# An attention and MoE kernel: the first loads in another order with filler matmuls, block means of v from two rows to a partition, q loaded in halves

## The chip, the core and the metric

The kernel runs on one core of a Trainium2 chip. The metric is device time in microseconds (us) of one execution. The core has four engines that compute (PE is TensorE, DVE is VectorE, ACT is ScalarE, POOL is GpSimd) and SyncE (SP), whose queue issues every load and store of this kernel to 16 DMA engines. Each engine takes its own instructions in a fixed order and waits where data or a buffer isn't ready.

## What is computed

Attention of 2 batches, 8 heads, 768 positions and 64 columns, in which a query sees the 31 keys around it and, for the rest, the 24 blocks of 32 keys: per block the maximum of k and the mean of v. Then two MoE-like layers on the 1536 tokens:

```python
k_sum = k.reshape(B, H, nb, block, D).max(axis=3)
v_sum = v.reshape(B, H, nb, block, D).mean(axis=3)
...
scores_s = scores_s + np.log(block)
...
scores_all = np.concatenate([scores_l_m, scores_s], axis=-1)
a = softmax(scores_all)
attn = np.matmul(a, np.concatenate([v, v_sum], axis=2))
# x: the attention's output, 1536 tokens x 512
h = x @ w_in                      # 512 -> 1024
x = layer_norm(h * softmax(h)) * g_ln @ w_out
h = x @ w_in2                     # 512 -> 2048
out = elu(h) @ w_out2
```

## The kernel before

The attention is done in 24 steps n (batch b, tile t of 64 queries, 12 tiles to a batch). For a step, `attn_s(n)` multiplies `q_bd[n]` (two heads on the diagonal of a 128 x 128 block, the other half zeros, so one matmul serves two heads) with the key window `kws[n % 4]` (96 keys and the 24 block maxima), adds a mask and takes the softmax: the sum with the mask and the minimum on DVE, the exponential on ACT, the scaling on POOL. `attn_p(n)` turns the result with PE transposes, and `attn_x(j)` multiplies the steps 2j and 2j+1 with their v windows `vws[n % 4]` (96 rows of v and the 24 block means) into `xT[j]`, 128 tokens for the first layer. `mm_in(j, n)` then runs the first layer's half n for these tokens: 4 slices of w_in, each with three matmuls (high parts, high by low, low by high), 12 matmuls to a half, written below as h(j, n). They need `xT[j]` and the slices of w_in, which arrive as 64-bit words and are turned into two 32-bit floats each by `convert`: ACT, POOL, DVE, DVE, ACT, DVE, one after the other; there are 8 slices, 0 to 3 for half 0, 4 to 7 for half 1. `lo_of`, the last DVE step of `convert` and of `split`, makes the low part; for `xT` it does so from PSUM.

The block maxima of k come from DVE reductions (`sum_k`), of batch 1 too. The block means of v come from matmuls (`sum_v`): six tiles of 128 rows of v, 512 columns in 32-bit floats, each multiplied with a slice of `avg` that puts four means in their rows; ACT brings the 24 x 512 result to `vsum`, and POOL copies it into each of the four v windows. Batch 1's v rows are loaded to a buffer that batch 0's v rows held before, and batch 1's keys (`load_k(1)`) go to that same buffer when the second `sum_v` has read it.

The order on SP is that of the program text (`manual_schedule`). PE, DVE, ACT and POOL are put in order by a scheduler at build time, which the text steers with priorities. SP has eight semaphores for its DMAs, taken in turn, so a load waits for the eighth one before it. In the beginning, 32 matmuls on zeros (`busy`) run while the first loads come.

## Time and profile before

| | us |
|---|---|
| median of 3 runs | 480.14 (479.35 to 481.42) |
| the profiled execution | 480.95 |
| its span, from the first to the last instruction | 479.2 |
| PE busy in the span | 464.0 (97%) |
| DVE, ACT, POOL busy | 298.6, 286.9, 122.3 |

The profiled execution's own time is 1.75 us over its span, and 0.81 us over the median. PE is busy for nearly the whole span, but the first instants hold fillers: the first matmul with data in it starts at 11.40 us.

### The profile page before, as it was taken

Reading aid. Unit: us, or ns where it says so; the run is one execution under the profiler, and the core shown is the slowest. Engines: PE = TensorE matmul, PEld = TensorE weight load, DVE = VectorE, ACT = ScalarE, POOL = GpSimd, SP = SyncE. Lnnn points to the kernel's source line nnn. Section 1 sums busy time; section 2 is a strip of 40 time slices with the busy share of each in tenths; the row PEclk is TensorE's granted clock in tenths of the full one; section 3 lists DMA queues with packets and bytes.
Section 4 is the critical chain, followed back from the end, with each engine's and each line's share of the span. In section 5 each row is a group of like instructions: output and inputs, shape, how many; then the busy total and the mean of one; then the engine's idle time right before and its main releaser. Section 6 shows DMA issues by size and latency. Waiting matters only on the chain.

```text
span 479.2 us, 7413 instructions
## 1 busy us (share of the span) xinstructions
PE 464.0 (97%) x2600; PEld 390.1 (81%) x2600; DVE 298.6 (62%) x664; ACT 286.9 (60%) x647; POOL 122.3 (26%) x213
## 2 busy tenths in 40 slices
PE   7789999899999999999999999999999999999996
PEld 3456788789988989999888888888888888888885
DVE  3786779885568529786998893367665565450000
ACT  1795697986568428475957673567667666560001
POOL 2795276755443512332222200000000000000000
PEclk9999999999999999999999999999999999999999
DMA  8996995462280543388879614442212222377112
GB/s 284 353 365 185 297 299 174 127 193 77 84 256 19 166 133 130 118 291 315 244 273 385 213 54 136 172 175 60 72 51 83 88 60 73 133 297 274 44 44 88
DMA packets 40116, 82.46 MB, mean 172 GB/s; under 512 B 9616, under 2 KB 18448, under 8 KB 40080
## 3 DMA queue, kind: packets, MB, share of 16 engines
q1 hardware_dynamic: 40080, 82.00, 52.1%
q8 instruction: 20, 0.33, 0.3%
q14 instruction: 16, 0.13, 0.1%
HBM read 70.46 MB, written 11.53 MB: 171 GB/s over the span
## 4 chain that ended last, share of the span: by engine, by line
PE 86%; DMA 8%; DVE 3%; ACT 1%; SPq 1%; issue 0%
PE o_ps L110 9%; PE o_ps L108 9%; PE o_ps L109 9%; PE h L110 7%; PE h L108 7%; PE h L109 7%; PE c L110 5%; PE c L108 5%; PE c L109 5%; DMA q_bd<-in_qd 5%; PE y_ps L108 5%; PE y_ps L110 5%; PE y_ps L109 5%; PE s_ps L218 3%; PE t_ps L299 2%; DMA vw<-in_v 2%
## 5 line engine op out<-in xcount | busy, mean ns | idle before, releaser
L129 POOL TENSOR_SCALAR conv<-conv 128x512 f32<-128x512 f32 x48 | 37.6, 785 | 81.2 <-ACT conv L126 79.6
L232 POOL TENSOR_SCALAR sm<-sm,st 128x120 f32<-128x120 f32 x96 | 43.8, 472 | 30.7 <-DVE st L230 14.3
L108 PE MATMUL o_ps<-w4r,g_hl 128*128 128x512 f32 x128 | 49.8, 389 | 0.0
L109 PE MATMUL o_ps<-w4r,g_hl 128*128 128x512 f32 x128 | 49.8, 389 | 0.0
L110 PE MATMUL o_ps<-w4r,g_hl 128*128 128x512 f32 x128 | 46.7, 389 | 0.0
L108 PE MATMUL y_ps<-lnT,w_out 128*128 128x384 f32 x128 | 43.6, 341 | 0.8 <-ACT y L316 0.8
L227 ACT ACTIVATE sm<-sm,st 128x120 f32<-128x120 f32 x96 | 37.0, 390 | 10.7 <-DVE st L224 10.7
L109 PE MATMUL y_ps<-lnT,w_out 128*128 128x384 f32 x128 | 43.2, 337 | 0.0
L110 PE MATMUL y_ps<-lnT,w_out 128*128 128x384 f32 x128 | 42.9, 336 | 0.0
L108 PE MATMUL h<-w_in,xT 128*128 128x512 f32 x96 | 39.3, 411 | 0.8 <-ACT xT L138 0.8
L110 PE MATMUL h<-w_in,xT 128*128 128x512 f32 x96 | 38.5, 401 | 0.8 <-DVE xT L105 0.8
L109 PE MATMUL h<-w_in,xT 128*128 128x512 f32 x96 | 38.4, 400 | 0.0
L224 DVE CUSTOM_DVE_ANT_0 sm<-s_ps,mask 128x120 f32<-128x120 f32 x96 | 21.6, 277 | 14.6 <-PE s_ps L218 14.2
L593 ACT ACTIVATE y<-y 128x512 f32<-128x512 f32 x48 | 30.0, 628 | 0.7
L621 DVE COPY y<-o_ps 128x512 f32<-128x512 f32 x5 | 3.5, 690 | 42.9 <-PE o_ps L110 42.9
L623 ACT ACTIVATE y<-o_ps 128x512 f32<-128x512 f32 x6 | 3.6, 600 | 43.9 <-PE o_ps L110 43.9
L105 DVE TENSOR_TENSOR g_hl<-y,g_hl 128x512 fp32r<-128x512 f32 x32 | 22.4, 701 | 11.3 <-ACT g_hl L138 11.2
L218 PE MATMUL s_ps<-kw,q_bd 128*128 128x120 f32 x192 | 25.9, 278 | 3.6 <-DMA q_bd<-in_qd 3.1
L218 PEld LDWEIGHTS s_ps<-kw,q_bd 128*128 128x128 f32 x192 | 23.9, 191 | 6.5 <-POOL kw L101 1.9
L109 PEld LDWEIGHTS o_ps<-w4r,g_hl 128*128 128x128 f32 x128 | 24.1, 188 | 5.1
L126 ACT ACTIVATE conv<-y 128x512 f32<-128x512 f32 x30 | 20.2, 676 | 13.3 <-DMA y<-in_w_in 11.3
L110 PEld LDWEIGHTS o_ps<-w4r,g_hl 128*128 128x128 f32 x128 | 24.0, 188 | 5.0
(148 smaller groups left out, 1239.9 us busy)
## 6 DMA issues: line engine op xcount, KB each, us to landing
w4r<-w4d SPq DMA_DIRECT2D x38, 512.0 KB, 3.4
y<-in_w_in SPq DMA_DIRECT2D x16, 512.0 KB, 5.9
w4d<-w3f SPq DMA_DIRECT2D x16, 512.0 KB, 3.4
y<-in_w_out SPq DMA_DIRECT2D x14, 512.0 KB, 7.0
q_bd<-in_qd SPq DMA_DIRECT2D x24, 256.0 KB, 7.0
bits<-in_w_out SPq DMA_DIRECT2D x10, 512.0 KB, 5.0
w4l<-w4d SPq DMA_DIRECT2D x10, 512.0 KB, 4.6
vw<-in_v SPq DMA_DIRECT2D x24, 192.0 KB, 6.5
```

The lines of the kernel that those rows point to most:

```text
L105: nc.vector.tensor_tensor(out_, x, hi.bitcast(F32), op=ALU.subtract)
L108: nc.tensor.matmul(ps, lhsT=l[0][ls], rhs=r[0][rs], start=first, stop=False, skip_group_check=parts)
L109: nc.tensor.matmul(ps, lhsT=l[0][ls], rhs=r[1][rs], start=False, stop=False, skip_group_check=parts)
L110: nc.tensor.matmul(ps, lhsT=l[1][ls], rhs=r[0][rs], start=False, stop=last, skip_group_check=parts)
L126: first = nc.scalar.activation(x, high.bitcast(F32), AF.Prelu, scale=TO_F32, alpha=SIGN_TO_28)
L129: nc.gpsimd.tensor_scalar(x, x, MOST, LEAST, op0=ALU.min, op1=ALU.max)
L218: nc.tensor.matmul(sps[:, p, 0:KW], lhsT=q_bd[n][:, p, :], rhs=kw[:, p, :], start=True, stop=True)
L224: nc.vector.tensor_tensor_reduce(sm[:, p, :], sps[:, p, 0:KW], mask[:, mi, :], -scale, 3.0e38, op0=ALU.add, op1=ALU.min, accum_out=nm[:, p ...
L227: nc.scalar.activation(sm[:, p, :], sm[:, p, :], AF.Exp, bias=nm[:, p:p + 1], scale=-1.0, accum_out=ss[:, p:p + 1])
L232: nc.gpsimd.tensor_scalar(sm[:, p, :], sm[:, p, :], ri[:, p:p + 1], 1.0, op0=ALU.mult, op1=ALU.mult)
L299: nc.tensor.transpose(tp[:, i, :], es[j][:, k * 128:(k + 1) * 128], ident)
L593: nc.scalar.activation(m, m, AF.Exp, scale=-1.0)
```

## The change

- **Loads.** SP's first loads are put in another order: batch 0's keys, q of step 0, the mask, q of step 1, then slices of w_in, v windows, `ident`, `avg` and v's rows between each other. Loading and converting a slice of w_in are now two functions (`words_w_in`, `convert_w_in`), and their places in the text are apart. `load_k(1)` stands two steps later in tick 1, behind the loads of that tick.
- **q.** The four q buffers are fixed tiles, whose zero halves VectorE writes once (8 memsets of 64 x 256). From step 2 on only the two non-zero quarters of a q block are loaded, as two DMAs of 64 partitions with runs of 64 floats (256 bytes) in place of one DMA with runs of 2 KB.
- **Means.** v's rows are loaded in three DMAs of 256 rows, two rows to a partition (runs of 4 KB) and not in six with runs of 2 KB; `avg` is loaded to match. Batch 0 still takes six matmuls. In batch 1 VectorE adds the two rows of each pair first (three additions of 128 x 512), and three matmuls are left. Batch 0's means go from PSUM straight into the first two v windows, one by ACT and one by DVE; POOL copies only into the other two.
- **Fillers.** 12 more matmuls on zeros follow the scores of step 1, and 7 follow `attn_x(0)`.

```diff
     def sum_v(b):
-        pst = psb.tile([128, DM], F32, tag="b", name="vs_ps")
...
-        for i in range(S // 128):
-            vt = v_sb[:, i * DM:(i + 1) * DM]
-            nc.sync.dma_start(vt, v[b, PAD + i * 128:PAD + (i + 1) * 128, :])
-            c0 = NB - i * 4
-            nc.tensor.matmul(pst, lhsT=avg[:, c0:c0 + 128], rhs=vt, start=i == 0, stop=i == S // 128 - 1)
-        vsum[b] = p_at.tile([128, DM], F32, tag="vsum", name="vsum", bufs=1)
-        nc.scalar.activation(vsum[b][WIN:KW, :], pst[WIN:KW, :], AF.Copy)
+        vts = [v_sb[:, i * 2 * DM:(i + 1) * 2 * DM].rearrange("p (s d) -> p s d", s=2) for i in range(S // 256)]
+        for i, vt in enumerate(vts):
+            nc.sync.dma_start(vt, v[b, PAD + i * 256:PAD + (i + 1) * 256, :].rearrange("(p s) d -> p s d", s=2))
+
+        def products():
+            pst = psb.tile([128, DM], F32, tag="b", name="vs_ps")
+            for i, vt in enumerate(vts):
+                c0 = NB - i * 8
+                if b:
+                    nc.vector.tensor_tensor(vt[:, 0], vt[:, 0], vt[:, 1], op=ALU.add)
+                for s in range(2 - b):
+                    nc.tensor.matmul(pst, lhsT=avg[:, c0:c0 + 128], rhs=vt[:, s], start=i + s == 0,
+                                     stop=i == S // 256 - 1 and s == 1 - b)
+            vsum[b] = p_at.tile([128, DM], F32, tag="vsum", name="vsum", bufs=1) if b else vws[0]
+            nc.scalar.activation(vsum[b][WIN:KW, :], pst[WIN:KW, :], AF.Copy)
+            if b == 0:
+                nc.vector.tensor_copy(vws[1][WIN:KW, :], pst[WIN:KW, :])
+        return products
...
     def load_q(n):
-        q_bd[n] = p_at.tile([128, NP, 2 * TQ], F32, tag="q", name="q_bd", bufs=4)
-        nc.sync.dma_start(q_bd[n], qd[n])
+        q_bd[n] = qs[n % NQ]
+        if n < 2:
+            nc.sync.dma_start(q_bd[n], qd[n])
+            return
+        for hh in range(2):
+            ds, cs = slice(hh * D, (hh + 1) * D), slice(hh * TQ, (hh + 1) * TQ)
+            nc.sync.dma_start(q_bd[n][ds, :, cs], qd[n, ds, :, cs])
...
+    keep_busy(32)
...
+    keep_busy(12, attn_s(1))
+    for i in range(2):
+        with tc.issue_after(marks[1, "max"].ins), tc.issue_after(marks[i, "exp"].ins):
+            convert_w_in(i)
+    means()
...
+    keep_busy(7, attn_x(0))
     attn_s(3)
...
         if t == 0:
-            sum_v(1)
-        elif t == 1:
-            load_k(1)
+            sum_v(1)()
...
             load_kw(s_n + 1)
+            if t == 1:
+                load_k(1)
             attn_s(s_n)
```

What this does to the engines' orders is seen best in the instructions as built. First SP's queue from its start, before; q_bd stands for the q of step 1 and then of step 0, vw_121 for the first v window, y_65 and y_66 for the places where slices of w_in arrive:

```order
L171 DMA k_sb<-in_kT 128x800 x4
L194 DMA q_bd<-in_qd 128x512
L198 DMA vw_121<-in_v 96x512
L474 DMA mask<-in_mask 128x360
L476 DMA ident<-in_ident 128x128
L194 DMA q_bd<-in_qd 128x512
L117 DMA y_65<-in_w_in 128x1024
L479 DMA avg<-in_avg 128x152
L117 DMA y_65<-in_w_in 128x1024
L186 DMA v_sb<-in_v 128x512 x6
L117 DMA y_66<-in_w_in 128x1024 x2
L194 DMA q_bd<-in_qd 128x512
```

And the same place in the changed kernel, where q_bd_126 to q_bd_129 are the four q buffers:

```order
L506 DMA avg<-in_avg 64x152
L507 DMA avg<-in_avg 64x148
L196 DMA v_sb<-in_v 128x1024 x3
L124 DMA y_66<-in_w_in 128x1024
L224 DMA vw_122<-in_v 96x512
L124 DMA y_66<-in_w_in 128x1024
L220 DMA q_bd_128<-in_qd 64x4x64 x2
L220 DMA q_bd_129<-in_qd 64x4x64 x2
L224 DMA vw_123<-in_v 96x512
L124 DMA y_67<-in_w_in 128x1024
```

The q of step 2 (q_bd_128) has moved behind the second v window and comes in two DMAs, the one of step 3 follows at once; ahead of this piece stand the keys, both first q, the mask, two slices of w_in, one v window and `ident`.

Next PE where the means of batch 1 are made, before. s_ps are scores, p_ps transposes, h the first layer, x_ps the product with v, kw_119 the key window of step 6:

```order
L188 MATMUL vs_ps<-v_sb,avg 128x512 x2
L108 MATMUL h<-w_in_89,xT 128x512
L188 MATMUL vs_ps<-v_sb,avg 128x512
L109 MATMUL h<-w_in_90,xT 128x512
L110 MATMUL h<-w_in_89,xT 128x512
L188 MATMUL vs_ps<-v_sb,avg 128x512 x3
L108 MATMUL h<-w_in_89,xT 128x512
L218 MATMUL s_ps<-kw_119,q_bd 128x120 x4
L254 MATMUL x_ps<-pT,vw_124 64x64 x8
```

And after:

```order
L205 MATMUL vs_ps<-v_sb,avg 128x512
L116 MATMUL h<-w_in_90,xT 128x512
L117 MATMUL h<-w_in_89,xT 128x512
L265 MATMUL p_ps<-ident,sm 120x128 x3
L205 MATMUL vs_ps<-v_sb,avg 128x512
L115 MATMUL h<-w_in_89,xT 128x512
L244 MATMUL s_ps<-kw_119,q_bd_128 128x120 x4
L205 MATMUL vs_ps<-v_sb,avg 128x512
L116 MATMUL h<-w_in_90,xT 128x512
L117 MATMUL h<-w_in_89,xT 128x512
L282 MATMUL x_ps<-pT,vw_124 64x64 x8
```

Three products are left of six, and the last of them now stands behind the scores of step 6.

Last DVE at the same place after the change, where L203 are the additions of v's pairs, L112 on w_in_90 the end of a slice's conversion, L137 and L141 steps of the next slices:

```order
L203 TENSOR_TENSOR v_sb<-v_sb 128x512
L112 TENSOR_TENSOR w_in_90<-conv,w_in_89 128x512
L137 TENSOR_SCALAR conv<-conv 128x512
L203 TENSOR_TENSOR v_sb<-v_sb 128x512
L141 SCALAR_TENSOR_TENSOR conv<-y_65,conv 128x512
L255 TENSOR_SCALAR st<-st 128x4
```

The three additions have come in between the conversions of slices 5, 6 and 7; the third stands behind the minimum of step 4's scores.

## Rows read from the trace of the kernel before

**Rows 1.** The page's first part: busy us, share of the span, instructions.
```profile
PE 464.0 (97%) x2600; PEld 390.1 (81%) x2600; DVE 298.6 (62%) x664; ACT 286.9 (60%) x647; POOL 122.3 (26%) x213
```
**Rows 2.** Busy us by stages; behind the engines the clock, DMA share, GB/s.
```profile
10.00:26.70 16.70, 11.76 (x84) 7.92 (x85) 11.46 (x48) 11.60 (x38) 13.36 (x25) 1.00 1.05 367
26.70:46.50 19.80, 17.76 (x115) 12.66 (x115) 14.23 (x50) 13.80 (x44) 15.78 (x29) 1.00 0.77 258
46.50:60.00 13.50, 13.04 (x125) 10.70 (x125) 10.25 (x40) 8.83 (x32) 3.66 (x12) 1.00 1.05 295
60.00:80.00 20.00, 19.88 (x134) 16.94 (x135) 16.35 (x54) 19.15 (x56) 16.02 (x31) 1.00 0.96 274
80.00:100.00 20.00, 18.30 (x164) 15.59 (x163) 16.91 (x60) 17.32 (x55) 13.03 (x24) 1.00 0.28 84
```
**Rows 3.** PE in order of time: start us, us, what, idle time before it.
```profile
1.17 8.82 PE L467 MATMUL busy<-ln 128*128 128x512 bf16 x32 [1.17 <-DVE ln L464]
11.40 2.02 PE L218 MATMUL s_ps<-kw,q_bd 128*128 128x120 f32 x16 [1.41 <-DMA q_bd<-in_qd]
14.89 1.95 PE L188 MATMUL vs_ps<-v_sb,avg 128*128 128x512 f32 x4 [1.47 <-DMA v_sb<-in_v]
22.38 1.12 PE L218 MATMUL s_ps<-kw,q_bd 128*128 128x120 f32 x8 [1.22 <-DMA q_bd<-in_qd]
26.70 0.50 PE L108 MATMUL h<-w_in,xT 128*128 128x512 f32 x1 [0.83 <-ACT xT L138]
41.25 1.15 PE L254 MATMUL x_ps<-pT,vw 120*64 120x64 f32 x32
46.51 0.50 PE L110 MATMUL h<-w_in,xT 128*128 128x512 f32 x1 [0.58 <-DVE xT L105]
54.33 0.40 PE L110 MATMUL h<-w_in,xT 128*128 128x512 f32 x1
```
**Rows 4.** The chain that ended last, from 28 to 41 us: start us, us, what.
```profile
28.15 0.23 PE h L108
...
37.63 2.59 PE vs_ps L188 x6
...
40.23 0.33 SPq L171
```
**Rows 5.** DVE in order of time, from 29 to 51 us.
```profile
29.46 0.69 DVE L105 TENSOR_TENSOR w_in<-conv,w_in 128x512 fp32r<-128x512 f32 x1 [0.98 <-ACT w_in L138]
34.04 0.97 DVE L105 TENSOR_TENSOR w_in<-conv,w_in 128x512 fp32r<-128x512 f32 x1
38.76 0.69 DVE L105 TENSOR_TENSOR w_in<-conv,w_in 128x512 fp32r<-128x512 f32 x1 [0.70 <-ACT w_in L138]
43.57 0.95 DVE L176 TENSOR_REDUCE ksum<-k_sb 128x24 f32<-128x768 f32 x1 [1.31 <-DMA k_sb<-in_kT]
45.77 0.68 DVE L105 TENSOR_TENSOR xT<-x_ps,xT 128x512 fp32r<-128x512 f32 x1
50.30 0.68 DVE L105 TENSOR_TENSOR w_in<-conv,w_in 128x512 fp32r<-128x512 f32 x1
```
**Rows 6.** DMA packets, MB, share of 16 engines: 15 to 20, then 110 to 120 us.
```profile
q1 hardware_dynamic: 808, 2.00, 103.9%
DMA packets 571, 0.29 MB, mean 29 GB/s; under 512 B 531, under 2 KB 531, under 8 KB 569
q1 hardware_dynamic: 569, 0.27, 9.1%
```
**Rows 7.** Issue of q for steps 7 and 6, then what the latter took to land.
```profile
31.41 2.28 SPq L194 DMA_DIRECT2D q_bd<-in_qd  x2
q_bd<-in_qd SPq DMA_DIRECT2D x1, 256.0 KB, 5.2
```
**Rows 8.** POOL in order of time: copies of the means, two stretches of scaling.
```profile
21.50 3.14 POOL L101 TENSOR_SCALAR vw<-vsum 24x512 f32<-24x512 f32 x4 [0.34 <-ACT vsum L190]
34.46 5.57 POOL L232 TENSOR_SCALAR sm<-sm,st 128x120 f32<-128x120 f32 x8
```

More of the change, by code (lines that the diff above doesn't have):

```diff
@@ L40 @@
 NCOPY = 12
+NQ = 4
 NG = 4
@@ L96, in tile_kernel @@
     avg = p_at.tile([128, 128 + NB], F32, name="avg", bufs=1)
+    qs = [p_at.tile([128, NP, 2 * TQ], F32, name=f"q_bd{i}", bufs=1) for i in range(NQ)]
+    zero = ln_t[:, 4, 0:256].bitcast(BF16)
+    nc.vector.memset(ln_t[:, 4, 0:256], 0.0)
+    for t in qs[2:] + qs[:2]:
+        for hh in range(2):
+            nc.vector.memset(t[hh * D:(hh + 1) * D, :, (1 - hh) * TQ:(2 - hh) * TQ], 0.0)
     nc.gpsimd.memset(negh, -0.5)
@@ L152, in tile_kernel, with words_w_in, convert_w_in @@
     early = stage[0] + stage[1] + stage[2]
-    def load_w_in(n, k):
+    def words_w_in(i):
+        n, k = divmod(i, KD)
+        load_words(early[i % 6], w_in[k * 128:(k + 1) * 128, n * 512:(n + 1) * 512].bitcast(I32))
+    def convert_w_in(i):
+        n, k = divmod(i, KD)
         cs = slice(n * 512, (n + 1) * 512)
-        convert(early[(n * KD + k) % 6], w_in[k * 128:(k + 1) * 128, cs].bitcast(I32),
-                w_in_hl[0][:, k, cs], w_in_hl[1][:, k, cs])
+        convert(early[i % 6], None, w_in_hl[0][:, k, cs], w_in_hl[1][:, k, cs])
     def load_w_out(k):
@@ L163, in convert_w_out @@
         convert(early[k % 6], None, *w_out_hl[k], gT[:, k:k + 1], pin=True)
-    k_sb, q_bd, xT, live, ksum, vsum = {}, {}, {}, {}, {}, {}
+    k_sb, q_bd, xT, live, ksum, vsum, marks = {}, {}, {}, {}, {}, {}, {}
     def load_k(b):
@@ L217, in attn_s @@
         for p in range(NP):
-            nc.tensor.matmul(sps[:, p, 0:KW], lhsT=q_bd[n][:, p, :], rhs=kw[:, p, :], start=True, stop=True)
+            last = nc.tensor.matmul(sps[:, p, 0:KW], lhsT=q_bd[n][:, p, :], rhs=kw[:, p, :], start=True, stop=True)
         sm = p_at.tile([128, NP, KW], F32, tag="sm", name="sm", bufs=NBUF)
@@ L233, in attn_s @@
         live[n] = sm
+        return last
     def attn_p(n):
@@ L247, in attn_x @@
             b, t = divmod(n, NT)
-            if t < NV:
+            if (b or t > 1) and t < NV:
                 copy_pool(vws[n % NV][WIN:KW, :], vsum[b][WIN:KW, :])
@@ L260, in attn_x @@
             for args in todo_x[1:]:
-                product_x(*args)
+                last = product_x(*args)
         for half in range(2):
@@ L264, in attn_x @@
         split(*xT[j], xps)
+        return last
     hs, es = {}, {}
@@ L436, in forms_late @@
         yf["B22"] = form("y1", b22)
-    conv = [lambda n=n, k=k: load_w_in(n, k) for n in range(2) for k in range(KD)]
     words = [lambda k=k: load_w_out(k) for k in range(KF1)]
     parts = [lambda k=k: convert_w_out(k) for k in range(KF1)]
-    def more(n=1):
-        for _ in range(n):
-            if conv:
-                conv.pop(0)()
     def mm_in(j, n):
@@ L460, in tr, with keep_busy @@
         ffn1_tr(j, 1)
-    zero = ln_t[:, 4, 0:256].bitcast(BF16)
-    nc.vector.memset(ln_t[:, 4, 0:256], 0.0)
     busy = psh.tile([128, F1], F32, tag="h", name="busy")
-    for i in range(32):
-        nc.tensor.matmul(busy[:, 0:512], lhsT=zero[:, 0:128], rhs=zero, start=True, stop=True)
+    def keep_busy(n, after=None):
+        with tc.issue_after(after.ins) if after else ExitStack():
+            with tc.high_priority():
+                for i in range(n):
+                    nc.tensor.matmul(busy[:, 0:512], lhsT=zero[:, 0:128], rhs=zero, start=True, stop=True)
+    keep_busy(32)
     loads = tc.manual_schedule(engines={mybir.EngineType.SP})
@@ L471, in tile_kernel @@
     load_k(0)
+    load_q(0)
+    nc.sync.dma_start(mask, mask_d)
     load_q(1)
+    words_w_in(0)
     load_v(0)
-    nc.sync.dma_start(mask, mask_d)
+    nc.sync.dma_start(ident, ident_d)
+    words_w_in(1)
+    nc.sync.dma_start(avg[0:64, :], avg_d.rearrange("(r two) c -> r two c", two=2)[:, 0, :])
+    nc.sync.dma_start(avg[64:128, 4:], avg_d.rearrange("(r two) c -> r two c", two=2)[:, 0, :124 + NB])
+    means = sum_v(0)
+    words_w_in(2)
+    load_v(1)
+    words_w_in(3)
+    load_q(2)
+    load_q(3)
+    load_v(2)
+    words_w_in(4)
+    load_v(3)
+    nc.sync.dma_start(gT, g_ln)
+    words_w_in(5)
     sum_k(0)
-    nc.sync.dma_start(ident, ident_d)
-    load_q(0)
-    more()
-    nc.sync.dma_start(avg, avg_d)
     attn_s(0)
-    more()
-    attn_s(1)
-    sum_v(0)
-    more(2)
+    keep_busy(12, attn_s(1))
[3 more added lines that the diff above has]
+    means()
+    convert_w_in(2)
+    convert_w_in(3)
     attn_p(0)
@@ L487, in tile_kernel @@
     attn_s(2)
-    load_v(1)
-    attn_x(0)
-    nc.sync.dma_start(gT, g_ln)
+    keep_busy(7, attn_x(0))
     attn_s(3)
-    load_v(2)
     attn_p(2)
+    words_w_in(6)
     attn_s(5)
-    more(3)
+    convert_w_in(4)
+    convert_w_in(5)
+    convert_w_in(6)
     attn_p(3)
+    words_w_in(7)
     attn_s(4)
-    load_v(3)
-    more()
+    convert_w_in(7)
     ticks = [(0, 0), (1, 0), (0, 1), (1, 1)] + [(j, n) for j in range(2, NJ) for n in range(2)]
```

5 lines of the change are left out of this document (3 added, 2 removed).

## The prediction

> **What bounds the kernel now.** I read the page's first part, then the busy time by stages, then PE in order of time, and at last the chain and the other engines around PE's gaps. PE is busy for 464.0 of 479.2 us [rows 1], so little beside PE's own work can be won, and only where PE idles or does work that counts for nothing. The stages say where that is [rows 2]: PE idles 4.9 us between 10 and 26.7 us (16.70 - 11.76), 2.0 us up to 46.5, 0.5 up to 60, 0.1 up to 80 and 1.7 up to 100. The fillers and the wait ahead of them fill the first 10 us [rows 3]. The granted clock is 1.00 in every stage, with these idle stretches in it, so TensorE already runs at 2.4 GHz and more fillers have no clock to win back.
>
> In order of time [rows 3], PE's stops are: for q of step 0 (until 11.40), for v's rows (until 14.89), for q of step 2 (until 22.38), for `xT` of the first 128 tokens (until 26.70, where the first layer begins) and for the low part of the second 128 tokens (until 46.51). The first three end by a load. In the same stages the 16 DMA engines are taken up: a share of 1.05 from 10 to 26.7 us [rows 2]. From 26.7 on, POOL is busy for 15.78 of 19.80 us, DVE for 14.23, ACT for 13.80 [rows 2]: here the conversions of w_in share three engines with the softmax.
>
> **The change, part by part.** *First scores.* The mask, one v window and `ident` no longer stand ahead of q of step 0, so the scores of steps 0 and 1 begin about when the 32 fillers end, at 10.0 (1.17 + 8.82, [rows 3]), not 11.40. That 1.4 us isn't kept: the next work needs v's rows, which have the same bytes ahead of them as before and now come 512 KB at a time. The 256 KB more cost 0.65 us at 2.00 MB in 5 us [rows 6], so the first product of means starts near 15.5, not 14.89. The 12 fillers take 12 x 0.23 us (a 512-column matmul, [rows 4]) = 2.8 and lie in that wait. Uncovered, that is a delay of 2.8 us.
>
> *Start of the first layer.* q of step 2 now stands behind another v window (192 KB, 0.5 us at the same rate), so I put its scores at 23.0, not 22.38. They take 1.1, `attn_x(0)` 1.15 (its 32 rows, [rows 3]), the 7 fillers 1.6, the scores of step 3 1.1: the first layer starts near 28.0 and not at 26.70, **1.3 us later**. Before, the scores of step 3 stood between the halves of `attn_x(0)`, and POOL's four copies of the means (3.14 us, [rows 8]) held those halves apart. Now ACT and DVE write the two first needed and POOL has 1.6 us less. I charge nothing for the late start further on: the first layer's fourth slice needs the conversion of slice 3, whose low part DVE began at 29.46 before [rows 5] and, with DVE's new order, begins near 30, so PE would stand there anyway. If that cover is gone, the 1.3 us is lost.
>
> *Means of batch 1.* Six products took 2.59 us for three [rows 4], so 0.86 each. Three are gone: **-2.6 us of PE**. DVE gets three additions of 128 x 512. Such an addition isn't in the trace; the nearest row is the low part of a conversion, the same size from two buffers, 0.68 to 0.97 [rows 5]. That makes 2.0 to 2.9 us in a stretch where DVE idles 5.6 of 19.8 [rows 2]. I take it as hidden, with 2.9 us as the other end.
>
> *What the saved products run into.* The last product of batch 1 frees the buffer for batch 1's keys. Before, the keys were issued at 40.23 when the last product ended [rows 4]; the first reduction of these keys began at 43.57, 3.3 us later, and took 0.95; behind it on DVE stands the low part of `xT` for the second 128 tokens, 45.77 plus 0.68, and PE stood until 46.51 for that [rows 3, 5]. In the new order of DVE the reduction still stands ahead of that low part. So this chain stays, and starts from the last product, which in PE's new order stands behind the scores of step 6. These need their q, which landed near 38.5 before (issued second in the row at 31.41, so near 33.3, plus 5.2, [rows 7]). I take 39.0 for it in the new order. Then: scores 1.0 to 40.0, product 0.86 to 40.9, keys 3.3 to 44.2, reduction 0.95 to 45.2, low part 0.7 to 45.9. PE goes on there **0.6 us earlier** than at 46.51. By the two orders PE has done 26 matmuls of the first layer ahead of that point, where before it had done 23, since slice 7 is converted earlier: three more at 0.23 are **0.7 us**. Together 1.3 us ahead at that point. So of the 2.6 us about half goes into this wait and the later start.
>
> *q in halves.* Bytes halve, packets go from 128 to 512 for a step. A step of 2 KB packets costs 0.68 us of the 16 engines (128 x 85 ns / 16, where 85 ns is 2 KB at 103.9% of 16 engines x 5 us for 2.00 MB, [rows 6]). Runs of 256 bytes are not in the trace. The nearest are the 384-byte runs of the key windows: from 110 to 120 us, 569 packets, 531 of them under 512 bytes, took 9.1% of 160 us, so 26 ns each [rows 6], and 512 of these are 0.82 us. I take this, so halving the bytes neither gains nor loses much (0.1 us a step). The bounds are 0.34 us by bytes alone and 2.7 us if any packet costs 85 ns. The Trainium skill ("DMA: Bandwidth & Descriptors", Specifications) says that below 512 bytes a transfer loses the line rate, since the engine reads, modifies and writes. The trace's 26 ns for 384 bytes, where the rate of the 2 KB packets would give 16, agrees in its sign; what the rule could do at its worst is the third rival.
>
> *Small things.* The 8 memsets of 64 x 256 are at most 0.3 us each and end ahead of the first keys; the extra SP issues stand where SP waits for landings anyway.
>
> *Later.* The first layer's last triple for the first tokens ended near 54.7 before, since slice 7's low part came at 50.30 [rows 3, 5]. By the new order it stands ahead of all of the second tokens' work, some 10 us earlier, so the first layer norm starts earlier and takes load from DVE and ACT, which are nearly full from 60 to 100 (ACT 19.15 of 20, [rows 2]). PE idles 2.3 us between 46.5 and 100 (0.5 + 0.1 + 1.7); I take 1.3 us of that, somewhat over half, as won, with 0 and 2.3 as the ends.
>
> **Sum.** 1.3 + 1.3 = 2.6 us: a span of 476.6 for 479.2. With the 1.75 us around the span that is 478.35 for the profiled execution; it lay 0.81 us over the median, so **477.5 us** against 480.14.
>
> **Rivals.** *1. VectorE takes the gain.* The additions come between the conversions of slices 5, 6 and 7, and if DVE has no gap there, 2.0 to 2.9 us push the last product, the keys behind it and slice 7. For it: three engines are 70 to 80% busy in the stage [rows 2]. Against it: DVE idles 5.6 us of it. Then 2.6 less 2.0 to 2.9, near 480.
>
> *2. All idle time goes.* If loads and conversions run ahead, PE stays full from 28 us on: 2.6 + 2.0 + 2.3 less 1.3 for the late start = 5.6, so 474.5. For it: slices of w_in are asked for earlier, and slice 7 no longer comes at 50. Against it: the chain over batch 1's keys.
>
> *3. The short runs of q cost more (the slower side).* Six steps' q (2 to 7) lie ahead of the scores of step 6, and in the stage from 46.5 to 60 us DMA is full again (1.05, [rows 2]). Each nanosecond over 26 a packet delays step 6 by 6 x 512 / 16 = 0.19 us. At 40 ns the gain of 2.6 is gone, and from there on the kernel is slower: at 55 ns 5.6 us less 2.6, so near 483. For it: nothing here shows 256-byte runs in a full queue. Against it: 26 ns in the stretch with the key windows. If reading and writing back each cost a 512-byte move of 21 ns (a quarter of 85), a packet is 42 ns, the six steps 3.1 us later and the time near 480.5. That is the worst that the skill's rule named above would do.
>
> **Chances.** The forecast, a gain of 1.2 to 4.2 us, 0.49; rival 1 0.18; rival 2 0.14; rival 3 0.19. A measurement of this kernel tells about 0.5% from no change, here 2.4 us. Three fifths of the forecast's range (1.8 of 3.0 us) lie beyond that (0.30) and two fifths within (0.19). Faster: 0.30 + 0.14 = 0.44. Same: 0.19 + 0.18 + 0.05 of rival 3 = 0.42. Slower: the other 0.14. The forecast's own range is 475.9 to 478.9. The range from 474.2 to 481.6 takes in rival 2 and the near part of rival 3.
>
> **What the profile after would show.** Right: fillers inside waits for v and for `xT`; three products of 0.86 us; the third behind the scores of step 6 near 40; the first layer's second tokens going on near 46 with a wait for DVE; q landings no longer than before; less than 1.7 us of idle PE from 80 to 100. Wrong: PE waiting at the products for the additions (rival 1), no wait for the low part of `xT` at all (rival 2), or PE's scores waiting for q from 30 us on (rival 3).

## The result and the profile after

The changed kernel takes **482.66 us** (median of 8 executions, 480.74 to 485.25), the kernel before 479.52 in the same comparison: a ratio of 1.0062, 95% interval 1.0046 to 1.0077. Two more measurements gave 1.0081 (1.0059 to 1.0104) and 1.0078 (1.0053 to 1.0102). The change costs 3.1 to 4.6 us in these three; 477.5 was forecast, and 481.6 was the end of the range.

The profiled execution took 481.76 us, with a span of 480.0. PE is busy for 1.6 us more than before [rows 1], although 2.6 us of products are gone, since 19 fillers have come (12 of 2.75 us together, 7 of 1.68, in PE's rows below). The page's first part:

```profile
PE 465.6 (97%) x2613; PEld 389.7 (81%) x2613; DVE 304.6 (63%) x676; ACT 286.8 (60%) x647; POOL 118.5 (25%) x211
```

The stages of [rows 2] again, with busy us of PE, PEld, DVE, ACT and POOL, then the clock, DMA share and GB/s:

```profile
10.00:26.70 16.70, 14.31 (x96) 8.56 (x95) 9.75 (x39) 10.21 (x30) 10.67 (x21) 1.00 1.05 329
26.70:46.50 19.80, 17.30 (x120) 12.29 (x119) 17.43 (x63) 14.93 (x52) 16.97 (x29) 1.00 0.80 250
46.50:60.00 13.50, 13.27 (x101) 11.07 (x100) 10.99 (x41) 10.21 (x38) 5.31 (x13) 1.00 1.02 290
60.00:80.00 20.00, 19.48 (x161) 16.22 (x161) 16.96 (x52) 17.71 (x53) 15.62 (x33) 1.00 0.75 213
80.00:100.00 20.00, 18.00 (x167) 15.38 (x166) 17.73 (x59) 18.26 (x56) 12.68 (x22) 1.00 0.48 131
```

From 26.7 to 46.5 us DVE has gone from 14.23 to 17.43 us and POOL to 16.97, and PE stands for 2.5 us where it stood for 2.0. From 60 to 100 us PE stands for 2.5 us, before for 1.8. PE in order of time, at the places of [rows 3] and at the three products:

```profile
9.69 1.94 PE L244 MATMUL s_ps<-kw,q_bd 128*128 128x120 f32 x16
11.47 2.75 PE L492 MATMUL busy<-ln 128*128 128x512 bf16 x12
15.56 1.96 PE L205 MATMUL vs_ps<-v_sb,avg 128*128 128x512 f32 x4 [1.34 <-DMA v_sb<-in_v]
22.87 1.12 PE L244 MATMUL s_ps<-kw,q_bd 128*128 128x120 f32 x8 [1.05 <-DVE vw L210]
25.01 1.68 PE L492 MATMUL busy<-ln 128*128 128x512 bf16 x7
27.34 0.48 PE L115 MATMUL h<-w_in,xT 128*128 128x512 f32 x1
35.92 0.32 PE L265 MATMUL p_ps<-ident,sm 128*120 128x128 f32 x1 [1.06 <-POOL sm L258]
39.73 1.05 PE L244 MATMUL s_ps<-kw,q_bd 128*128 128x120 f32 x8
40.62 1.03 PE L205 MATMUL vs_ps<-v_sb,avg 128*128 128x512 f32 x2
43.70 0.32 PE L265 MATMUL p_ps<-ident,sm 128*120 128x128 f32 x1 [0.51 <-POOL sm L258]
47.09 0.50 PE L117 MATMUL h<-w_in,xT 128*128 128x512 f32 x1 [0.23 <-DVE xT L112]
90.25 0.32 PE L265 MATMUL p_ps<-ident,sm 128*120 128x128 f32 x1 [1.34 <-POOL sm L258]
```

The scores begin at 9.69, v's rows at 15.56, the scores of step 2 at 22.87, all near the forecast; the wait ahead of the latter ends with DVE's copy of the means (L210). New are three waits for POOL's scaling (1.06, 0.51 and 1.34 us; before's longest of this kind, up to 100 us, is 0.18). The second tokens go on at 47.09, 0.6 us later than before and not earlier.

Where the time goes shows in the start of five pieces of PE's work (us, from PE's order of time; "before, 2nd" and "after, 2nd" and "3rd" are the traces of e2, e9 and e1 below):

| | first h | first t_ps | first y_ps | second layer | span |
|---|---|---|---|---|---|
| before | 26.70 | 74.83 | 100.80 | 224.58 | 479.2 |
| before, 2nd | 26.65 | 73.29 | 99.25 | 223.02 | 477.6 |
| after | 27.34 | 73.52 | 100.41 | 224.25 | 480.0 |
| after, 2nd | 27.58 | 74.05 | 100.88 | 224.68 | 479.7 |
| after, 3rd | 28.73 | 76.33 | 103.18 | 227.00 | 483.1 |

The first layer starts 0.6 to 2.1 us later. From first h to first t_ps, where the products are saved, the first two traces of after take 46.2 and 46.5 us, before 48.1 and 46.6. From t_ps to y_ps all three of after take 26.8 to 26.9, before 26.0 both times: 0.9 us lost. PE's listed waits there sum to 2.3 to 2.4 us in after and 1.7 before, where these two take the place of after's 1.34:

```profile
87.78 0.65 PE L237 MATMUL p_ps<-ident,sm 128*120 128x128 f32 x4 [0.81 <-DVE st L224]
90.54 1.15 PE L218 MATMUL s_ps<-kw,q_bd 128*128 128x120 f32 x8 [0.48 <-DVE st L224]
```

So about 0.7 of the 0.9 us are waits. From y_ps to the second layer nothing changes (123.8), and behind it 0.4 to 1.5 us go (254.6 us to the end before, 255.0 to 256.1 after; in the first trace 0.44 of it is a wait for DVE's `g_hl` at 272 us, and DVE had itself waited 2.10 us at 270.59 for a store to `w4d`).

### The profile page after: what moved, and what is told of

Read it like the earlier page. It is cut to its first block, busy times and chain, and to the rows that moved or that the text cites. A ratio compares the mean times of both kernels' runs of the same rounds, so it can differ in the third digit from the quotient of the medians.

```text
span 480.0 us, 7478 instructions
## 1 busy us (share of the span) xinstructions
PE 465.6 (97%) x2613; PEld 389.7 (81%) x2613; DVE 304.6 (63%) x676; ACT 286.8 (60%) x647; POOL 118.5 (25%) x211
## 4 chain that ended last, share of the span: by engine, by line
PE 80%; DMA 9%; DVE 6%; issue 2%; POOL 1%; ACT 1%; SPq 0%
PE o_ps L117 8%; PE o_ps L116 8%; PE o_ps L115 8%; PE h L117 6%; PE h L116 6%; PE h L115 6%; PE c L117 5%; PE c L115 5%; PE c L116 5%; PE y_ps L115 5%; PE y_ps L117 5%; PE y_ps L116 5%; DMA y<-in_w_in 3%; PE s_ps L244 3%; PE t_ps L328 2%; DMA k_sb<-in_kT 2%
## 5 line engine op out<-in xcount | busy, mean ns | idle before, releaser
L136 POOL TENSOR_SCALAR conv<-conv 128x512 f32<-128x512 f32 x48 | 35.0, 729 | 84.6 <-ACT conv L133 83.4
L258 POOL TENSOR_SCALAR sm<-sm,st 128x120 f32<-128x120 f32 x96 | 42.5, 461 | 22.5 <-DVE st L256 15.0
L112 DVE TENSOR_TENSOR g_hl<-y,g_hl 128x512 fp32r<-128x512 f32 x32 | 22.9, 716 | 10.5 <-ACT g_hl L145 10.4
L117 PEld LDWEIGHTS o_ps<-w4r,g_hl 128*128 128x128 f32 x128 | 24.0, 188 | 5.8 <-DVE g_hl L112 0.9
L116 PEld LDWEIGHTS o_ps<-w4r,g_hl 128*128 128x128 f32 x128 | 24.1, 188 | 5.0
L115 PEld LDWEIGHTS o_ps<-w4r,g_hl 128*128 128x128 f32 x128 | 24.0, 188 | 5.0
```

Of the source, the lines that this page charges most:

```text
L112: nc.vector.tensor_tensor(out_, x, hi.bitcast(F32), op=ALU.subtract)
L115: nc.tensor.matmul(ps, lhsT=l[0][ls], rhs=r[0][rs], start=first, stop=False, skip_group_check=parts)
L116: nc.tensor.matmul(ps, lhsT=l[0][ls], rhs=r[1][rs], start=False, stop=False, skip_group_check=parts)
L117: nc.tensor.matmul(ps, lhsT=l[1][ls], rhs=r[0][rs], start=False, stop=last, skip_group_check=parts)
L136: nc.gpsimd.tensor_scalar(x, x, MOST, LEAST, op0=ALU.min, op1=ALU.max)
L258: nc.gpsimd.tensor_scalar(sm[:, p, :], sm[:, p, :], ri[:, p:p + 1], 1.0, op0=ALU.mult, op1=ALU.mult)
```

## Experiments

Each is given as the median and the ratio to the kernel before in the same comparison.

**e1_after_again and e2_before_again**: both kernels unchanged.

> The changed kernel again, for the spread from execution to execution and a second trace. Theory A (the short runs of q make loads late, and by a different amount each time): about 1.006 of before, spans from 479 to 483.5, and in the trace a wait for q, v or k that the first trace did not have. Theory B (the new order of DVE and POOL puts waits between 30 and 48 us and again between 60 and 100): 1.006 too, but the waits of the first trace again, POOL's scaling ahead of the transposes first among them. Theory C (TensorE's clock falls in some executions): granted clocks under 1.00, and the lower the clock, the longer the span.

> The kernel before as a kernel of its own, for the span and clock of each of its executions. All theories: ratio 1.000, spans within 2 us of each other. Theory C: clocks of 1.00 in all of them. If clocks below 1.00 show here too at the same times, theory C falls.

484.78 (1.0081), and 480.23 (0.9998, 0.9983 to 1.0012): a comparison of a kernel with itself is good to 0.15%. All six executions of e1 had a mean granted clock of 0.996 or less; in the first measurement it was 3 of 8, in e9 5 of 9. The trace of e1 shows a fall of the clock that before's two traces do not have. PE in stretches of 2 us (busy us, clock, DMA share, GB/s):

```profile
34.00:36.00 2.00, 1.57 (x9) 1.00 1.03 386
36.00:38.00 2.00, 0.80 (x5) 0.87 1.08 262
38.00:40.00 2.00, 2.00 (x8) 0.50 0.38 88
40.00:42.00 2.00, 2.00 (x8) 0.78 0.28 64
42.00:44.00 2.00, 2.00 (x12) 1.00 0.01 2
```

PE waited 0.43 us and then 1.20 us for POOL's scaling (at 34.96 and 37.30); the clock then fell to 0.50, 1.2 GHz, and was back at 2.4 GHz by 42 us. Three stretches at 0.87, 0.50 and 0.78 lose 2 x (0.13 + 0.50 + 0.22) = 1.7 us.

**e3_whole_q**: the changed kernel, q loaded as before; only SP's queue differs.

```diff
         q_bd[n] = qs[n % NQ]
-        if n < 2:
-            nc.sync.dma_start(q_bd[n], qd[n])
-            return
-        for hh in range(2):
...
+        nc.sync.dma_start(q_bd[n], qd[n])
```

> All q loads in one DMA of 128 partitions with runs of 2 KB, all else as changed; only SP's queue differs. Theory A: the loss goes, 0.995 to 1.001 of before and the spread is as narrow as before's. Theory B: 1.005 to 1.007 as the changed kernel, since the other engines' orders are the same. Theory C: as the changed kernel.

482.90 (1.0045, 1.0027 to 1.0064), 1.9 us under e1 in the same comparison. Part of this is the clock: only 4 of the 7 executions of e3 had a mean of 0.996 or less (median 483.2, the others 481.9), against all six of e1. Beside the changed kernel's medians at either level (484.6 and 482.3, below) q whole is worth 0.4 to 1.4 us, so only a part of the loss goes. SP's issue of slice 4 of w_in is at 17.38 us where e1 has 20.60. In this trace the clock fell behind the wait for POOL's scaling near 90 us:

```profile
90.00:92.00 2.00, 0.66 (x4) 0.83 0.81 255
92.00:94.00 2.00, 2.00 (x12) 0.50 0.05 11
```

**e4_no_fillers**: the changed kernel without its 19 new fillers (the scheduler gives the other engines a new order too).

```diff
-    keep_busy(12, attn_s(1))
+    attn_s(1)
...
-    keep_busy(7, attn_x(0))
+    attn_x(0)
```

> The 12 and the 7 fillers left out, the 32 at the start kept; the scheduler then changes the order of PE, DVE and ACT near them. Prediction's term: the 12 lie in the wait for v and cost nothing, the 7 hold back the first layer by 1.3 to 1.6 us, of which nothing is lost later; so 0 to 1.6 us faster than the changed kernel (1.003 to 1.006 of before). Theory C: if the fillers hold the clock, granted clocks fall here and the time rises above the changed kernel's.

484.96 (1.0095, 1.0076 to 1.0113). PE waits 4.3 us for v's rows, and the clock is 0.50 from 16 to 20 us: the fillers filled that wait. The time is that of e1 (484.78), five of its executions have a clock of 0.995 or less, and the order is new: what the fillers keep of the clock here and what they cost elsewhere is not told apart.

**e5_pairs_alone, e18_pairs_again**: the kernel before, with the pairs of batch 1 and nothing else of the change.

```diff
+        vts = [v_sb[:, i * 2 * DM:(i + 1) * 2 * DM].rearrange("p (s d) -> p s d", s=2) for i in range(S // 256)]
+        for i, vt in enumerate(vts if b else []):
+            nc.sync.dma_start(vt, v[b, PAD + i * 256:PAD + (i + 1) * 256, :].rearrange("(p s) d -> p s d", s=2))
+        for i, vt in enumerate(vts if b else []):
+            c0 = NB - i * 8
+            nc.vector.tensor_tensor(vt[:, 0], vt[:, 0], vt[:, 1], op=ALU.add)
+            nc.tensor.matmul(pst, lhsT=avg[:, c0:c0 + 128], rhs=vt[:, 0], start=i == 0, stop=i == S // 256 - 1)
-        for i in range(S // 128):
+        for i in range(0 if b else S // 128):
...
     load_v(3)
+    nc.sync.dma_start(avg[0:64, :], avg_d.rearrange("(r two) c -> r two c", two=2)[:, 0, :])
+    nc.sync.dma_start(avg[64:128, 4:], avg_d.rearrange("(r two) c -> r two c", two=2)[:, 0, :124 + NB])
```

> The kernel before with one part of the change: v's rows of batch 1 come two to a partition, VectorE adds the pairs and three products make the means (the table of means is loaded a second time for it, 78 KB). PE's order differs from before in the places of these products alone. By the prediction's working, the three saved products (2.6 us of PE) are worth what the chain over batch 1's keys lets through: 0.6 to 2.6 us, so 477.6 to 479.6 where before takes 480.2. If VectorE takes the gain (rival 1), 480 to 481. If the change's loss lies in this part, it takes more than 481.

> The kernel before with the pairs for batch 1 alone, a second time: 478.5 to 479.3, about 1 us under before, if the first measurement (0.9982 of before, interval to 1.0) was no chance; within 0.3 us of before if it was.

478.82 (0.9982, 0.9964 to 1.0) and 479.95 (0.9986, 0.9971 to 1.0001): some 0.8 us under before both times, each interval just reaching it. In e5 PE waits for each of the additions:

```profile
34.96 1.12 PE L190 MATMUL vs_ps<-v_sb,avg 128*128 128x512 f32 x2 [0.59 <-DVE v_sb L189]
36.89 1.12 PE L190 MATMUL vs_ps<-v_sb,avg 128*128 128x512 f32 x2 [0.29 <-DVE v_sb L189]
38.25 1.12 PE L190 MATMUL vs_ps<-v_sb,avg 128*128 128x512 f32 x2 [0.23 <-DVE v_sb L189]
```

That is 1.1 of the 2.6 us, a share of rival 1.

**e6_six_products**: the changed kernel with six products and no additions.

```diff
-                if b:
-                    nc.vector.tensor_tensor(vt[:, 0], vt[:, 0], vt[:, 1], op=ALU.add)
-                for s in range(2 - b):
+                for s in range(2):
```

> The changed kernel with six products for batch 1's means and no additions on VectorE. If the additions are what costs time (rival 1), this gains 2 to 2.9 us on VectorE's path and gives back 2.6 us of PE: 482 to 484, no slower than the changed kernel (483 to 485). If the three saved products are worth their PE time, it takes 1.3 to 2.6 us more than the changed kernel: 485 to 487.

484.06 (1.01, 1.0079 to 1.0122). That lies between the two expectations (the upper end of the first, below the second), in a new order of the engines. Taking the additions out gains nothing clear of noise, so they are not seen to cost the changed kernel its time; without the additions the rest of the change loses 4 to 5 us.

**e7_no_second_fillers**: the changed kernel without `keep_busy(7, ...)`.

> The changed kernel without the 7 fillers behind the first xT (the 12 stay). If they only delay the scores of step 3 and with them the first layer, the first layer starts 0.8 us earlier (near 26.5 us in the trace) and the kernel gains 0.5 to 1 us: 482.5 to 484 where the changed kernel takes 483 to 485. If they hold the granted clock up, the clock falls near 26 to 32 us and the kernel loses 1 to 2 us.

480.53 (1.0019, 0.9998 to 1.004), by the ratios 2 to 3 us less than the changed kernel. Its trace is of one of the 5 executions of 12 with a fall of the clock (482.4 us): the clock is 0.81, 0.50 and 0.84 from 24 to 30 us, behind a wait of 1.88 us for step 2's q, and the first layer starts at 29.01 us. The scheduler has moved work on four engines here; from first h to t_ps it takes 45.7 us.

**e8_fill_at_90**: the changed kernel with 10 fillers in the wait near 90 us, into a half of h that is written later; no other order changes.

```diff
+        if (j, n, k) == (5, 0, 0):
...
+            with tc.issue_after(b.ins), tc.high_priority():
+                for i in range(10):
+                    nc.tensor.matmul(hs[j][:, 512:768], lhsT=iw[:, 0:128], rhs=iw, start=True, stop=True)
```

> The changed kernel with 10 fillers of 256 columns (1.1 us) in PE's wait for POOL's scaling near 90 us; no other engine's order changes, and the fillers' results are overwritten. If falls of the granted clock behind this wait cost the changed kernel time in part of its executions, the mean clock no longer falls under 0.997 from there, and the median gains 1 to 2 us: 482 to 483. If the loss is in the order of work alone, the time stays that of the changed kernel (483 to 485) or grows by up to 0.3 us.

481.72 (1.0043, 1.0025 to 1.0061), by the ratios 0.9 to 1.8 us under the changed kernel. The fillers leave 0.24 us of that wait, and the clock stays up there:

```profile
90.00:92.00 2.00, 1.49 (x11) 1.00 0.31 79
92.00:94.00 2.00, 1.76 (x16) 1.00 0.56 192
```

3 of its 11 executions had a mean clock of 0.996 or less (the unchanged one: 14 of 23). In the traced one it fell at another place (0.62 and 0.53 from 26 to 30 us), behind 2.31 us of waiting for step 2's q.

**e9_after_third, e10_fillers_ahead_of_s2, e11_combined**: the changed kernel; the same with its 7 fillers ahead of step 2's scores; that with q whole, step 2's q asked for ahead of the second v window and of slice 3 of w_in, and e8's fillers.

```diff
-    attn_p(1)
+    keep_busy(7, attn_p(1))
     attn_s(2)
-    keep_busy(7, attn_x(0))
+    attn_x(0)
```

> The changed kernel unchanged, as the reference of this call. Theory: its loss is the sum of a later start of the first layer (0.6 to 2 us), an order near 75 to 100 us that costs 0.9 us more, and falls of the granted clock to 0.50 behind an idle stretch of PE, 2 us each, in over half of its executions; the pairs give back about 1 us. So 482.5 to 485, with runs of mean clock 0.997 and less among them that are slower than the others. Rival: the loss is the same in every execution and the clock has no part in it; then the runs at 0.998 and above are as slow as the others.

> The changed kernel with its 7 fillers (1.6 us) moved from behind the first x_ps to ahead of step 2's scores, where PE waits 1.0 to 2.3 us for that step's q. If the place behind x_ps only delays the scores of step 3, the gain of the kernel without the 7 fillers (about 2 us) stays, and the fall of the clock that its trace showed at 24 to 30 us goes: 479 to 480.5, and no granted clock under 0.9 from 24 to 32 us. If the 7 fillers' gain was an accident of the new order, it stays with the changed kernel at 482 to 485.

> As the last, and with three more edits: q whole as before (1.0 to 1.5 us less in the pair of runs above), q of step 2 asked for ahead of the second v window and of slice 3 of w_in (1.7 us of queue), and 10 short fillers in the wait near 90 us. If the losses are those of the theory and add up, 477.5 to 479.5, under before. If the order near 75 to 100 us and the three engines' load set the time whatever the start does, 480 to 481.5.

483.78 (1.0078), 484.40 (1.0094, 1.0065 to 1.0122), 482.39 (1.0049, 1.003 to 1.0069). Moving the fillers gained nothing, against the expectation. It fits the rival, by which e7 gains by its new order and not by a place freed on PE; but e10 has an order of its own too, and all six of its executions have a clock of 0.996 or less, so this is argued and not shown. e11's time is above both of its expectations. In e11 the earlier q pushed slice 3 back, and ACT's order has slice 3's conversion ahead of `xT`. ACT and then PE:

```profile
28.90 0.66 ACT L133 ACTIVATE conv<-y 128x512 f32<-128x512 f32 x1 [1.83 <-DMA y<-in_w_in]
29.47 0.58 ACT L145 ACTIVATE xT<-x_ps 128x512 fp32r<-128x512 f32 x1
30.10 0.50 PE L115 MATMUL h<-w_in,xT 128*128 128x512 f32 x1 [2.77 <-ACT xT L145]
```

The wait for q was turned into a longer one for a load that ACT waits for, and the clock is 0.62 and 0.52 from 30 to 34 us behind it. Behind a wait of PE for `xT` (1.59 us) e10 has its clock at 0.50 to 0.52 from 30 to 36 us.

**e12_pairs_and_fillers**: e5 with 5 fillers in the wait for v and 4 in the wait for step 2's q; no other instruction moves.

> The kernel with the pairs alone, with 5 fillers in its wait for v's rows and 4 in its wait for step 2's q, about 0.4 us shorter than the waits; no other instruction moves. If the falls of the clock (3 of its 12 runs had a mean of 0.996 and less, about 1 us slower) begin in these two waits, they go, and the median falls by 0.2 to 0.4 us to 478.4 to 478.6. If they begin elsewhere, it stays at 478.8; if fillers overrun their waits, up to 0.5 us more.

479.74 (0.9992, 0.9973 to 1.0012): no gain over the pairs alone (0.9982 and 0.9986). 3 of its 12 executions still had a mean clock of 0.996 or less, as in e5, so filling these two waits does not keep the falls away.

**e13_q_halves_alone, e17_q_two_whole_issues**: the kernel before with q in halves, or with two transfers of 64 partitions that keep the 2 KB rows. PE, ACT and POOL keep before's order; DVE gains the 8 memsets.

```diff
-        nc.sync.dma_start(q_bd[n], qd[n])
+        for hh in range(2):
+            ds, cs = slice(hh * D, (hh + 1) * D), slice(hh * TQ, (hh + 1) * TQ)
+            nc.sync.dma_start(q_bd[n][ds, :, cs], qd[n, ds, :, cs])   # e13
+            nc.sync.dma_start(q_bd[n][ds], qd[n, ds])                 # e17
```

> The kernel before with one part of the change: q of step 2 on in halves, into four tiles that are cleared at the start (8 memsets). The order of PE, ACT and POOL is that of before, DVE's gains the memsets alone. By the prediction (26 ns a packet of 256 bytes) it is neutral within 0.5 us: 479.5 to 480.5. If the halves are what the changed kernel lost against the same with whole q (1.9 us between the medians), 481 to 482, with waits of PE's scores for q or later landings of the transfers that share the queue, in the first 60 us.

> As the kernel with the halves of q alone, but each of a step's two transfers takes 64 partitions with their whole rows of 2 KB (zeros too): two issues a step as there, the 128 packets of 2 KB of before. SP's orders differ in nothing else. If the number of issues and of outstanding transfers is what costs, 481 to 482.5, as with the halves (482.2 where before took 479.7). If the 256-byte runs cost (0.6 us on SP for an issue of 256 runs where one of 128 long ones takes 0.33, and 28 ns for each packet), 479.5 to 480.5, as before, and w_in's later slices are asked for no more than 1 us later than before.

482.19 (1.0046, 1.0026 to 1.0065) and 485.68 (1.0105, 1.0084 to 1.0126). So the halves alone cost 2.5 us, and without the short runs two transfers cost 5.6, above both of e17's expectations: the short runs are not needed for a loss. (e17's trace is of its fastest execution, 482.93 us at a clock of 1.00, and shows 2.8 of the 5.6 us; 4 of its 6 executions had 0.996 or less.) SP in order of time (issue at, us until issued), from e2:

```profile
14.84 0.33 SPq L194 DMA_DIRECT2D q_bd<-in_qd  x1
18.28 0.33 SPq L194 DMA_DIRECT2D q_bd<-in_qd  x1
19.49 2.88 SPq L117 DMA_DIRECT2D y<-in_w_in  x3
```

From e13:

```profile
15.58 1.53 SPq L205 DMA_DIRECT2D q_bd<-in_qd  x2
23.18 1.19 SPq L205 DMA_DIRECT2D q_bd<-in_qd  x2
24.41 1.56 SPq L123 DMA_DIRECT2D y<-in_w_in  x3
```

From e17:

```profile
14.75 1.18 SPq L205 DMA_DIRECT2D q_bd<-in_qd  x2
21.55 1.10 SPq L205 DMA_DIRECT2D q_bd<-in_qd  x2
22.70 1.53 SPq L123 DMA_DIRECT2D y<-in_w_in  x3
```

Step 2's q is issued at 14.84, 15.58 and 14.75 us, but step 5's 3.3 to 4.9 us later than in e2, and with it slices 4 to 6 of w_in (3.2 and 4.9 us). Both kernels start behind e2: SP waits for the 8 memsets (2.8 us together) and issues the first q at 3.95 us where e2 has 2.57; by step 2's q e17 has made this up, and e13 is 0.74 us late. What SP waits for there, from e13's waits of SP between 12 and 26 us (us in total, times, longest):

```profile
SPq L205 <- DMA y<-in_w_in: 2.2, 1, 2.2
```

Each transfer takes one of SP's eight semaphores in turn. With two transfers for each q, step 5's q stands eight places behind slice 3 and waits for it to land, and slices 4 to 6 stand behind that. The two issues themselves take 1.1 to 1.2 us of SP without a wait, where one takes 0.33. The queue as a whole (packets, MB, share of 16 engines), from the pages of e2, e13 and e17 in turn:

```profile
q1 hardware_dynamic: 40080, 82.00, 51.4%
```

```profile
q1 hardware_dynamic: 48880, 79.12, 51.7%
```

```profile
q1 hardware_dynamic: 40432, 82.00, 54.1%
```

Times 16 spans that is 3928 us of engine time in e2 (3940 to 3995 in the traces of before, e5, e12 and e18, with whole q too), 3979 in e13, 4164 in e17. e17 moves the same bytes and needs 169 to 236 us more. The trace times every packet: those of 2 KB, q's 2816 among 8320, took 113.0 ns on average in e17, 105.3 in before and 102.8 in e2, which is 64 to 85 us of it; the 384-byte packets of the key windows took 31.8 ns where they took 23.4 to 24.3, another 46 to 52 us. The rest lies in the other packets, within what whole-q traces differ by. Where q's were the only 2 KB packets under way, a packet took 127 ns in e17 (issued at 124.66 us) and 84 in before and e2 (at 122.48 and 120.92), though at a second such place it was 102.5, against 136 and 112. In the pages of e2 and e17 (KB of a transfer, median us until it lands):

```profile
q_bd<-in_qd SPq DMA_DIRECT2D x24, 256.0 KB, 6.9
```

```profile
q_bd<-in_qd SPq DMA_DIRECT2D x44, 128.0 KB, 6.1
```

Half the bytes land in nearly the same time. The Trainium skill ("SBUF — State Buffer", Door 1: The DMA port swizzle) says why that may be: partitions 0 to 63 reach only 8 of SBUF's 16 DMA ports, and (in "Can I just issue two DMAs to hit both halves?") two transfers into the two halves do not make up for it. The trace of e17 agrees in sign (113.0 ns for a 2 KB packet, before 105.3); no run shows the ports.

**e14_whole_q_no_second_fillers, e15_pairs_direct_means, e16_loads_and_fillers_alone**: e3 and e7 together; e5 with batch 0's means written straight to the first two v windows; the changed kernel with q whole, six products and POOL's copies as before (v's rows still two to a partition, the memsets and the later `load_k(1)` kept).

```diff
-        vsum[b] = p_at.tile([128, DM], F32, tag="vsum", name="vsum", bufs=1)
+        vsum[b] = p_at.tile([128, DM], F32, tag="vsum", name="vsum", bufs=1) if b else vws[0]
...
+        if b == 0:
+            nc.vector.tensor_copy(vws[1][WIN:KW, :], pst[WIN:KW, :])
...
-            if t < NV:
+            if (b or t > 1) and t < NV:
```

> The changed kernel with whole q and without the 7 fillers behind the first x_ps; order of PE, DVE, ACT and POOL as in the kernel without the 7. If both losses are real and add (about 2 us each against 483 to 485), 478 to 480, no slower than before. If the two are the same loss, or one of them was chance, 480.5 to 482.

> The kernel before with two parts of the change: the pairs for batch 1, and batch 0's means written by ACT and DVE straight to the first two v windows. If the direct means take POOL's copies (1.6 us) off the way of the first xT, the first layer starts up to 0.8 us earlier than with the pairs alone (26.9 us) and the kernel takes 478 to 479. If DVE's copy only comes in the way of its conversions, or the new order of DVE and ACT costs as much, 479 to 480.5.

> The changed kernel with what is left when the pairs, the direct means and the halves of q are taken back: the order of the first loads and conversions and the 19 fillers alone. If this part holds the bulk of the loss (first layer later by 0.6 to 2 us, 0.9 us near 75 to 100 us, falls of the clock), 482 to 484, and PE begins y_ps 26.8 us after t_ps and not 26.0. If the halves of q and the direct means hold it, 480 to 481.5.

480.90 (1.0021, 1.0003 to 1.0039), 480.47 (1.0019, 1.0003 to 1.0035), 480.83 (1.0018, 0.9998 to 1.0039). e14 shows that the losses of e3 and e7 are not independent: together they gain no more than e7's edit alone. e15: the direct means take the pairs' gain away and more. In its trace PE waits 1.19 and 0.49 us for additions, at products that in e5 waited 0.59 and 0.29. e16: the new order of the loads with its fillers loses about 0.9 us, an interval that just reaches none. Its first layer starts last of all (first h at 30.15 us) and yet t_ps comes at 73.48; y_ps is 26.5 us behind that.

## Why the prediction was wrong

**The sum of the parts.** Measured alone, in per cent of before: pairs -0.16 (mean of two), direct means on top of them +0.35, halves of q +0.46, loads and fillers +0.18. Together +0.83, and the change measured +0.62 to +0.81. The pairs fall out of this sum (it is e15, e13 and e16), each term is good to 0.2 and the sum to some 0.3, and the memsets are in two of the kernels. So the parts account for the loss within that, and the halves of q are about half of it; taken out of the change itself (e3), they are worth 0.36 of e1's 0.81, and less at a like clock. The kernels are separate ones, whose orders the scheduler made anew (in e13 and e3 it did not), so the terms of the direct means and of the loads hold for these orders only.

**The step that failed first** is under *Small things*: "the extra SP issues stand where SP waits for landings anyway". They do stand there, but each takes a semaphore, so the wait behind them is for a later landing: slice 4 of w_in is asked for 3.2 us later in e1 than in e3, 4.9 later in e13 than in e2. So the change does not ask for the late slices earlier (slice 4 at 19.70 us in after, 19.42 before), which *rival 2* counted on. In e13 ACT stands 1.57 us for a slice that lands at 30.58, and PE then waits 1.15 us for ACT's high part of w_in at 33.17. e13's loss lies ahead of t_ps (76.81 us, before 74.83 and 73.29); from there to y_ps it takes 26.0 us, as before. The same item has the memsets "at most 0.3 us each" and done ahead of the first keys: they took 0.35 each, and the first q waits for them, 0.7 us in after and 1.4 in e13 and e17.

**The first 1.3 us of the sum** did not come. By 47 us PE has done 26 matmuls where before had done 23, as forecast, but it goes on at 47.09, 0.6 us later than before, which leaves 0.1 of the 1.3. The list of before's stops there also left out the longest, which stands at the products, for DVE:

```profile
34.12 1.96 PE L188 MATMUL vs_ps<-v_sb,avg 128*128 128x512 f32 x4 [1.25 <-DVE st L230]
```

e5 does not have it, so its 1.1 us of waits for additions stand partly in its place.

**"q in halves ... neither gains nor loses much"** was right for the packets and wrong for the kernel. e13's queue took as much engine time as before's (3979 in 3928 to 3995); its 11,264 packets of 256 bytes took 21.0 ns on average, and I had taken 26. *Rival 3* had the right part and sign and the wrong mechanism: its 55 ns a packet did not come, its scores did not wait for q from 30 us on in the three traces of the changed kernel, and e17 loses more with no short runs at all. The Trainium skill's rule on 512 bytes ("DMA: Bandwidth & Descriptors", Specifications), weighed there, did not decide it. The rate of the 2 KB packets would give 10.6 ns for 256 bytes, so the 21.0 agree with its sign. The Trainium skill's rule on 64 partitions ("SBUF — State Buffer", Door 1: The DMA port swizzle), which I did not weigh, speaks against this part. In e13 the trace shows only the places on SP; whether slower landings have a part in its 2.5 us stays open.

**"TensorE already runs at 2.4 GHz and more fillers have no clock to win back"** held for the kernel before with the pairs: e12's fillers won nothing. It did not hold for the changed kernel. Of its 23 executions 14 had a mean granted clock of 0.996 or less, with a median of 484.6 us; the other 9 had 482.3. Of before's 137 it was 13, with 481.7 and 479.95. So some 2.3 us of the loss are there without a fall, and the falls add 2.4 us in half of the executions more than before, 1.2 us on average. The traces put them behind PE's waits for POOL's scaling (e1, e3), for step 2's q (e7, e8) or for `xT` (e10, e11). e8, whose fillers sit in one of these waits, keeps 1.00 there.

**"Later: 1.3 us won"**. 0.9 us were lost from t_ps to y_ps. The conversions did run earlier, as forecast (slice 7's low part at 42.25, before 50.30 [rows 5]), and the first layer norms came earlier (52.52, before 58.58). On DVE, whose rows here are of after, a step for `lnT` and the norm (1.9 us together) now stand between the two steps of a softmax; POOL's scaling comes behind them:

```profile
87.33 0.57 DVE L255 TENSOR_SCALAR st<-st 128x4 f32<-128x4 f32 x1
87.82 0.68 DVE L112 TENSOR_TENSOR lnT<-t_ps,lnT 128x512 fp32r<-128x512 f32 x1
88.42 1.21 DVE L312 SCALAR_TENSOR_TENSOR ln<-h,ln 128x1024 f32<-128x1024 f32 x1
89.56 0.17 DVE L256 RECIPROCAL st<-st 128x4 f32<-128x4 f32 x1
89.83 1.40 POOL L258 TENSOR_SCALAR sm<-sm,st 128x120 f32<-128x120 f32 x4 [1.94 <-DVE st L256]
```

POOL's scaling waits for that reciprocal, and PE for POOL until 90.25. Which part of the change makes this order stays open. The wait of 1.3 us (or the fillers in it) is in e3, e4, e6 to e11 and e14 too, and not in e5, e12, e13, e15, e16, e17 or e18. e16 has the early conversions and norms (53.61) without it, so these alone do not make it; nor do the direct means alone (e15). e6 has it without the additions and e3 without the halves. That leaves the direct means together with the new order of the loads, and no run takes the direct means alone out of the change.

**The chain over batch 1's keys** was right in its links and 1.2 us short in size. Scores of step 6 at 39.73 (39.0 taken), last product until 41.6 (40.9), keys issued at 41.68, reduction at 45.48 (44.2), low part at 46.35, PE at 47.09 (45.9). DVE and the issue of the keys:

```profile
45.48 0.95 DVE L187 TENSOR_REDUCE ksum<-k_sb 128x24 f32<-128x768 f32 x1 [0.57 <-DMA k_sb<-in_kT]
46.35 0.68 DVE L112 TENSOR_TENSOR xT<-x_ps,xT 128x512 fp32r<-128x512 f32 x1
41.68 2.43 SPq L182 DMA_DIRECT2D k_sb<-in_kT  x4
```

The keys took 3.8 us and not 3.3: four issues last 2.43 us here. The scores of step 6 wait for no q; PE only gets there then.

**What was right.** The first scores, v's rows, a first layer that starts later (1.3 us; 0.6 to 2.1 measured) and the size of the additions (0.67 to 0.80 us). They cost PE nothing in the changed kernel (no wait for them there), as forecast, but 1.1 us in e5. The saved products are worth 0.8 us alone, where 2.6 of PE are saved. *Rival 1* is thus right in part for the pairs, not for the change; *rival 2* didn't come. The sign "less than 1.7 us of idle PE from 80 to 100" came out wrong (2.0).
